# State attention with a gated projection: the scale of the scores moved into the exponentials, the order of all work remade

## Chip, cores, metric

One Trainium2 chip, one of its cores. The metric is device time of one execution in microseconds (us). The kernel before: 211.58 us, the median of 3 runs (211.08 to 211.69).

## What is computed

x is (8 batches, 8 heads, 512 tokens, 64), state is (8, 8, 32, 64), all in float32. Cut to what matters:

```python
scores  = (x @ state.T) / 8;  a  = softmax(scores);   xread = a  @ state     # per token, over 32 states
scores2 = (state @ x.T) / 8;  a2 = softmax(scores2);  sread = a2 @ x         # per state, over 512 tokens
x = concat([xread, sread], token axis)            # (8, 544, 512) after the heads are put side by side
gate = sigmoid(5-tap causal convolution of x over tokens, one weight per channel and tap)
out  = (gate * (x @ w_val)) @ w_out
```

(The reference's shapes give 512 + 32 tokens for each batch; `x` in the third line is reused for the concatenation.)

## The kernel before

Everything of one batch follows the same stages, and the stages of eight batches are interleaved. For batch b:

- `scores` (L347): PE multiplies the state, transposed (`sT`), with the tokens, transposed (`xT`), into two PSUM tiles `sc` (one for each half g of the heads). Each is 8 products on small parts of the array; a product in plain float32 leaves two records in the trace.
- The softmax over states: DVE transposes blocks of `sc` into `sl` (L400), takes the maximum `mx` (L410); POOL subtracts it (L221, `sl<-sl,mx`); ACT takes the exponential into `ex` (L417); DVE sums (`sm`) and inverts (`rc`); POOL multiplies (L221, `ex<-ex,rc`); DVE transposes back (L432) into `sl` (`a` for batch 0).
- The softmax over tokens: DVE takes the negated maximum `nb` straight from `sc` (`max_s`, L358); ACT takes `exp(sc + nb)` into `e2` (`exp_s`, L361). PE transposes `e2` (`exp_T`, tile `e2p`, L368), ACT or DVE copies it to `e2T`, PE multiplies with `x` (`state_read`, tile `srp`, L377), ACT divides (`sr`, L390), PE transposes (`srT`, L393) and ACT copies into `xt`, which the tail works on.
- `state_val` (tile `sgv`): state times `w_val` on PE, then `swh` and `swl`, a high and a low part that a fast matmul form can take. ACT makes the high part, DVE (`state_val_low`, L332) the low one.
- `read` (tiles `xr`, L439): PE makes the read of each of four channel groups; ACT, DVE and POOL make the five taps of the convolution (`acc`, `last`) and ACT the gate `sig`. For batch 0, PE does the taps (`read_conv`, L454, 80 records) from `z5`, which POOL makes from `z` and the taps.
- `values` (tiles `val`, L503): PE multiplies `ah`, `al` (high and low part of the softmax) with `swh`, `swl`. DVE makes `g = (sig + 1) * val` (L508), ACT or POOL its high part `gh` (L208, L212), POOL the low part `gl` (L221).
- `project` (tiles `op`, L512 to L514): three products of 512 columns for each of 4 x 4 pieces, with `woh` and `wol` (high and low part of `w_out`), copied to `o` and stored.

Weights arrive as float64 words; in the first 40 us ACT (`words_part` L279 `wt`, `words_side` L287 `ws`), POOL (`ws`, L289) and DVE (`words_sum`, L295 and L297; `words_join`, L304) turn them into float32, and ACT and POOL into `woh` and `wol`.

What the change is about: `sT`, the transposed state, is multiplied by 1/8 on ACT after it has landed (`state_T`, L316 to L318, three instructions), so that `sc` holds scaled scores, and the two places that use `sT` for `state_val` undo it with `HALF / SCALE` (L329, L333, L345).

```python
    def state_T(r, i0, i1):
        t = get("sT", r)[:, i0:i1]
        nc.scalar.mul(t, t, SCALE)
```

The order of the work is not left to a scheduler. The kernel lists its steps in `steps`; `ORDER` is a table of step numbers, in which a letter names the engine for steps that may run on ACT (a), DVE (v) or POOL (g). Each engine, and SP's DMA queue, runs its instructions in that order and waits in place. `SLOTS` names for each tile in turn the buffer that it takes; a buffer is written when its last reader is done, so a product on PE may wait for the engine that empties its PSUM tile (8 tiles, tag `ps`). `WARM` gives the numbers of filler products (`warm_up`, L314) at the start.

Of the kernel before, what the change touches and what calls it, by code (L numbers as in the profile page):

```python
# [8 lines left out]
F32 = mybir.dt.float32  # L9
F32R = mybir.dt.float32r  # L10
# [13 lines left out]
P = 128  # L24
# [5 lines left out]
PLAIN = (0,)  # L30
# [6 lines left out]
WARM = (9, 2, 14)  # L37
# [8 lines left out]
278 64a 146 168 288a 65g 147 279 187 135 274 129g 189 190 132a 275 133g 101 191 136 173a 148 193 276g 142 194 102a
199a 237 195 198 149 192a 200 137 196g 201 143 277 152 174g 197 153 284 205 202 154 144a 175 150a 155 207 138a 203g
219 208 156a 139 225 213a 209 151 226 282g 212 157 220 227 206a 214 238 204 221 215 285 228 294 210g 222 229a 216 378
223a 297a 217g 180 485 295a 380 181 145 286a 387 290 224g 182 389 289 388 298 183 239 184a 230g 218 379 231 291 232
240 390 299 283g 296 241a 381 211 292 233 293a 394 307 234 334 300 242g 309 328 395a 346 302 321 335 382g 310 329 301a  # L50
340 311 341 303 308a 347 336 323 383 312g 342 304 348 235a 324 243 305g 313 255 325 315a 384 330 236g 322a 256 314 244
326g 306 337 257 316 258 385g 331 245 393 332a 317 246 259a 318 333g 260 403 247a 386 377 338a 248 487 404a 339g 486
406a 396 703 489 327 249 319g 391a 498 250 405 499 251 392g 488 397a 252 349 320 407 261 253a 496 408 490 505 424a 343
262 506a 423 449 263 344a 425 264 345g 426 437 265a 427 438 409 352 428g 410a 439 416 411 450 491g 350a 353 412 497
354 418 429 364 419 351g 492 358 413 451 430 493 414g 365 417a 359 415 432 360 494g 433 366 420 361 431a 452 367 421g
362a 440 399 363 368a 434 398 495 112 435g 400 596 422 453a 512 812 605 441a 454g 369 597 401 515a 266 455 607 113a
456 500a 442g 355 516 436 598 443 606 501g 444 445 356a 457 402a 513a 446 357 503 608 458 517 447a 599 504a 614 448g
525 558 514 370 518 527 600g 532 461 615v 459a 371 528 533a 546 529 460g 372 534 526a 462 601 535 530g 547 536 373 520
467 537g 374a 502 564 521 375 559 538 560 539 468 561 519a 463 541 469 522 470 542 523g 464 540a 471a 507 543 465a 508
472 602 562a 544g 705 595 509 524 612 563g 706 929a 479 707 552 603g 714 548 510 553 549 554 716 550a 565 708 613a 566  # L60
551g 545 480 511a 611 715 473 604 531 481 567 474 609a 555 482 717 610g 475 927a 476 556a 483a 723 477a 621 484 557g
626 622a 709g 624a 623 617 634 625 616 724a 636 721 704 618 568g 655 478 627 637 667 466 641 629 656 569g 635a 588 630
710 668 631 589 722a 638 657 628a 643 619 669 933a 632g 661 644 931a 662 620a 711 663 639g 642a 590 633 591 720 648
712g 645 576 640 658 577 650 659a 726 646g 592a 651 725 664 814 727 813 660g 652 254 730 593 816 649a 815 728 731a 570
653g 823 729a 733a 571 825 824 572 817 826 573 647 713 578 665a 574a 579 666g 670 718a 735 734 580a 829 719g 732 830
736 581 832 671a 575 738 582 743 739 583 831a 818g 745 770 833a 771 654 740 673 757 746 584 737a 759 772 751a 741g 674
760 819 675 679 676 672g 742 764 744a 765 677a 691 747 750 761 766 748g 585 820 680 586a 678g 758a 692 752 749 681
762g 773 682 753 774a 685 821g 683a 767 693 754 684 768a 694 763 769g 822 839 695a 696 755g 835 827a 834 842a 844 775g
836 843 837 845 686 934g 852 687 847 840a 854 782 928g 756 783 848 838a 688 853a 841 828g 866 784 855 776 846a 785 777
689a 778 856 786a 690 697 937 779 587 857g 879 849 780a 891 938 868 892 932g 935a 885 869 880 860a 939 873 850g 858  # L70
886 881 787g 851 893 859 698 867a 936g 699 882 861 874 700 862 794 870 701a 781g 875 887 806 930g 876 807 863 877a
883a 788 940 878g 948 795 947 789 884g 950 942 941 871g 808 864g 949 943 952 944 951 872 953 945a 946g 800 954 801 894
955a 790 865 956g 796 921 895g 888 802 809 889a 896g 797 810a 922 890g 811 702 791 963 792a 957 909 803 958 804a 798a
964 799 965 793 923 805 966 959 967a 903 968 904 924 905 897 960 898 961a 910 925a 899 926 915 962 900 906 901a 911
902 907a 912 916 908 913a 917 918 914 919a 920
# [4 lines left out]
    "06126005634267501024315671027614305672465276124300127146753231763245041567746302041372520631672135460573642014"  # L80
    "375631520132715604234721237631500675123420124710253601714572056031437240534",
    x="0100101000",
    xT="01001001",
# [5 lines left out]
    ah="01001100101",
    al="0110011010",  # L90
    swh="0100110010",
    swl="011001101",
    acc="0120201221022011210102101202",
    last="0110100101011010011110110101",
    sig="00123323332233223333223332323322303",
    g="0101100110101001111010100101010101",
    gh="0011201100232231045210364126403514620153640",
    gl="01023121120345203164024361034261305241",
    o="0123030312111312320301003123020130",
    nb="00000000",  # L100
    r2="00100000",
    mx="00000000",
    sm="00000000",
    rc="00000000",
# [6 lines left out]
def state_attention_gated_kernel(  # L111
# [41 lines left out]
        sr=(1, [P, P], F32), sl=(2, [P, NG, S], F32),  # L153
# [3 lines left out]
        g=(2, [P, S], F32), gh=(7, [P, S], F32R), gl=(7, [P, S], F32R), o=(4, [P, C], F32),  # L157
        nb=(4, [P, NG], F32), r2=(2, [P, NG], F32),
# [33 lines left out]
    def op(fn, *args):  # L192
        steps.append((fn, args))
# [150 lines left out]
    def state_val_high_part(e, b, g, i):  # L344
        scale(e, get("sw0", b)[:, g, i * C // 2:(i + 1) * C // 2], get("sgv", b, g, i)[:, :C // 2], HALF / SCALE)  # L345
# [70 lines left out]
    def exp_n(b, i):  # L416
        nc.scalar.activation(part(ex, b, i)[..., :NS], blocks(get("sl", b), b, i), AF.Exp)  # L417
# [208 lines left out]
    def batch(b):  # L626
# [171 lines left out]
```

## Time and profile before

| what | value |
|---|---|
| median of 3 runs | 211.58 us |
| the profiled execution, its own time | 212.08 us |
| its span, first to last instruction | 209.9 us |
| PE busy | 203.2 us, 97% of the span, 1781 matmul records |
| DVE, ACT, POOL busy | 159.4, 155.2, 152.5 us (76%, 74%, 73%) |
| granted PE clock, mean | 0.997 of full speed |
| moved by DMA | 31.24 MB, 149 GB/s |

Matmul records overlap: the next one starts while the last one drains, and the ends are modelled. A product of 512 columns in the fast form has a duration of about 0.39 us, yet the next one starts some 0.23 us after it. So what PE can do is read from start to start, and a short wait shows as a longer step, not as idle time. ACT, DVE and POOL columns are plain busy time.

### The profile page before, as it was taken

To read this page: it belongs to the slowest core of one execution; us is meant where nothing else is said; L and a number is where in the kernel's file an instruction comes from. 1 tells how busy PE (TensorE), PEld (TensorE's weight loads), DVE (VectorE), ACT (ScalarE), POOL (GpSimd) and SP (SyncE) were. 2 spreads that over 40 slices of the span, in tenths; PEclk is the share of its full clock that TensorE was granted. 3 is DMA by queue.
4 is the path that set the end of the run, shared out by engine and by line. 5 is a ranking of instruction groups with operands and counts; after the bars stand their busy time and mean duration, and the time that the engine had idled before them with its cause. 6 is when DMAs were issued, how large, how long until landed. Compare 5 with 4: busy or idle time off the path is not lost.

```text
span 209.9 us, 4603 instructions
## 1 busy us (share of the span) xinstructions
PE 203.2 (97%) x1781; PEld 147.0 (70%) x1781; DVE 159.4 (76%) x255; ACT 155.2 (74%) x325; POOL 152.5 (73%) x118
## 2 busy tenths in 40 slices
PE   7799999999999999999999999999999999999994
PEld 6654457676688567766777857577866788988883
DVE  1799999998999988998969759998895988630000
ACT  3498999977987978789755989799879964333123
POOL 2286999999979938988938596948799999473000
PEclk9999999999999999999999999999999999999998
DMA  6999689604700692048016028182011200002525
GB/s 182 417 370 425 263 248 425 284 0 153 253 0 2 187 415 100 0 101 303 0 55 250 3 62 279 25 286 103 0 52 53 101 0 3 0 0 100 186 79 188
DMA packets 9507, 31.24 MB, mean 149 GB/s; under 512 B 1146, under 2 KB 1678, under 8 KB 7566
## 3 DMA queue, kind: packets, MB, share of 16 engines
q1 hardware_dynamic: 9342, 30.43, 39.9%
q10 hardware_dynamic: 144, 0.52, 1.0%
q8 instruction: 14, 0.23, 0.4%
q14 instruction: 7, 0.06, 0.1%
HBM read 22.04 MB, written 8.91 MB: 147 GB/s over the span
## 4 chain that ended last, share of the span: by engine, by line
PE 86%; DVE 4%; issue 1%; ACT 1%; ACTq 0%
PE val L503 21%; PE op L512 13%; PE op L514 13%; PE op L513 13%; PE srp L377 4%; PE e2p L368 4%; PE xr L439 3%; PE sgv L324 3%; PE tval L580 3%; PE sc L353 3%; DVE acc L483 2%; PE xr L454 2%; PE top L513 1%; PE top L514 1%; PE top L512 1%
## 5 line engine op out<-in xcount | busy, mean ns | idle before, releaser
L483 DVE SCALAR_TENSOR_TENSOR acc<-xr,cwt,acc 128x511 f32<-128x511 f32 (+2 forms) x84 | 60.3, 741 | 6.0 <-ACT last L216 2.4
L512 PE MATMUL op<-woh,gh 128*128 128x512 f32 x124 | 50.1, 404 | 0.2 <-DVE acc L483 0.2
L514 PE MATMUL op<-woh,gl 128*128 128x512 f32 x124 | 49.1, 396 | 0.0
L513 PE MATMUL op<-wol,gh 128*128 128x512 f32 x124 | 48.9, 394 | 0.0
L221 POOL TENSOR_TENSOR gl<-g,gh 128x512 fp32r<-128x512 f32 x32 | 41.2, 1295 | 7.7 <-ACT gh L208 7.5
L221 POOL TENSOR_TENSOR acc<-acc,last 128x508 f32<-128x508 f32 x28 | 35.9, 1286 | 12.8 <-DVE acc L483 7.0
L512 PEld LDWEIGHTS op<-woh,gh 128*128 128x128 f32 x124 | 23.4, 189 | 6.3 <-issue 0.6
L514 PEld LDWEIGHTS op<-woh,gl 128*128 128x128 f32 x124 | 23.3, 188 | 5.6 <-POOL gl L221 0.3
L513 PEld LDWEIGHTS op<-wol,gh 128*128 128x128 f32 x124 | 23.3, 188 | 5.0 <-issue 0.2
L208 ACT CAST gh<-g 128x512 fp32r<-128x512 f32 x30 | 18.7, 632 | 10.1 <-DVE g L508 8.0
L208 ACT COPY o<-op 128x512 f32<-128x512 f32 (+1 forms) x33 | 18.4, 579 | 10.1 <-PE op L514 8.3
L508 DVE SCALAR_TENSOR_TENSOR g<-sig,val 128x512 f32<-128x512 f32 x32 | 21.3, 675 | 5.7 <-POOL tgl L221 1.5
L216 ACT ACTIVATE last<-xr,cwt 128x508 f32<-128x508 f32 x28 | 19.7, 708 | 6.5 <-DVE acc L483 5.0
L221 POOL TENSOR_TENSOR sl<-sl,mx 128x1024 f32<-128x1024 f32 (+1 forms) x9 | 15.6, 1729 | 7.3 <-DVE mx L410 7.2
L495 ACT ACTIVATE sig<-acc 128x512 f32<-128x512 f32 x28 | 17.9, 641 | 2.6 <-POOL acc L221 2.6
L478 ACT ACTIVATE acc<-xr,cwt 128x512 f32<-128x512 f32 x28 | 19.3, 708 | 0.7 <-PE xr L439 0.5
L221 POOL TENSOR_TENSOR al<-sl,ah 128x1024 fp32r<-128x1024 f32 x7 | 16.9, 2413 | 2.5 <-ACT ah L208 2.3
L503 PE MATMUL val<-ah,swh 128*128 128x512 f32 x56 | 17.2, 403 | 0.0
L503 PE MATMUL val<-al,swh 128*128 128x512 f32 x56 | 17.1, 395 | 0.0
L503 PE MATMUL val<-ah,swl 128*128 128x512 f32 x56 | 16.7, 397 | 0.4 <-issue 0.4
L221 POOL TENSOR_TENSOR ex<-ex,rc 128x1024 f32<-128x1024 f32 (+1 forms) x9 | 15.6, 1729 | 1.6 <-DMA z<-z_in 0.9
L332 DVE SCALAR_TENSOR_TENSOR swl<-sgv,swh 128x512 fp32r<-128x512 f32 x14 | 9.3, 676 | 5.5 <-ACT swh L216 5.5
(120 smaller groups left out, 378.3 us busy)
## 6 DMA issues: line engine op xcount, KB each, us to landing
x<-x_in SPq DMA_DIRECT2D x8, 1024.0 KB, 7.2
out<-o SPq DMA_DIRECT2D x31, 256.0 KB, 2.3
xT<-xT_in SPq DMA_DIRECT2D x7, 1024.0 KB, 10.9
vw<-w_val SPq DMA_DIRECT2D x4, 511.8 KB, 9.4
ow<-w_out SPq DMA_DIRECT2D x4, 511.8 KB, 5.2
xT<-xT_in ACTq DMA_DIRECT2D x1, 512.0 KB, 4.8
xT<-xT_in SPq DMA_DIRECT2D x1, 512.0 KB, 5.3
z<-z_in SPq DMA_DIRECT2D x2, 256.0 KB, 7.9
```

The source lines that it names most:

```text
L208: nc.scalar.copy(out, in_)
L216: nc.scalar.mul(out, in_, factor)
L221: (nc.vector if e == "DVE" else nc.gpsimd).tensor_tensor(out, a, b, op=how)
L332: nc.vector.scalar_tensor_tensor(get("swl", b)[:, g], get("sgv", b, g), HALF / SCALE, get("swh", b)[:, g].bitcast(F32), op0=ALU.mult, op1= ...
L478: nc.scalar.mul(get("acc", b, pr), pt, cw[:, HALO, pr:pr + 1])
L483: nc.vector.scalar_tensor_tensor(acc[:, d:], get("xr", b, pr)[:, :S - d], cw[:, HALO - d, pr:pr + 1], acc[:, d:], op0=ALU.mult, op1=ALU.add)
L495: nc.scalar.activation(get("sig", b, pr), get("acc", b, pr), AF.Tanh, scale=0.5)
L503: nc.tensor.matmul(get("val", b, k), w[:, g, c], a[:, g], start=(term == 0 and g == 0), stop=(term == terms - 1 and g == NG - 1))
L508: nc.vector.scalar_tensor_tensor(get("g", b, k), get("sig", b, k), 1.0, get("val", b, k), op0=ALU.add, op1=ALU.mult)
L512: nc.tensor.matmul(pt, gh, woh[:, k], start=(k == 0), stop=False)
L513: nc.tensor.matmul(pt, gh, wol[:, k], start=False, stop=False)
L514: nc.tensor.matmul(pt, gl, woh[:, k], start=False, stop=(k == NPR - 1))
```

## The change

- The three multiplications of `sT` go. `sc` now holds unscaled scores; both exponentials on ACT take `scale=SCALE` (1/8) with their input, and the three uses of `HALF / SCALE` become `HALF`.
- The exponential over tokens needs its bias scaled as well: a new step `bias_s` makes `ns = nb / 8`, one value for each partition, two for each batch. The table puts 13 of these 16 steps on POOL and 3 on DVE.
- `SLOTS` gives the buffers nearly always in turn; `sr` has 2 buffers instead of 1, `g` 3 instead of 2, `o` 8 instead of 4, and `ns` 4.
- On SP's queue the weight loads ahead of `x` of batch 0 come in the order `vw` 3, `ow` 3, `vw` 2, `ow` 0; before it was `ow` 3, `ow` 0, `vw` 3, `vw` 2.
- `ORDER` is remade throughout. The 25 filler products, before in groups of 9, 2 and 14, stand in groups of 9, 2, 5, 6, 1 and 2.

```diff
-WARM = (9, 2, 14)
+WARM = (9, 2, 5, 6, 1, 2)
...
-68 15 0 8 69 20 25 158 2 6 1 55 40 9 969 71 10a 35 11 74 73 12 75 970 72 30 81 13 76g 14a 82 22a 91 70 77 83 21 78 84g
...
+65 12 0 5 66 17 22 157 1 3 32 52 982 68 6 7a 27 71 70 8 72 983 69 37 9 79 73g 78 18 89 67 74 80 984 10 15 90g 11a 16a
...
-    sr="00000000",
-    sl="00101010",
+    sr="01010101",
+    sl="01010101",
...
-        sr=(1, [P, P], F32), sl=(2, [P, NG, S], F32),
+        sr=(2, [P, P], F32), sl=(2, [P, NG, S], F32),
...
-        g=(2, [P, S], F32), gh=(7, [P, S], F32R), gl=(7, [P, S], F32R), o=(4, [P, C], F32),
-        nb=(4, [P, NG], F32), r2=(2, [P, NG], F32),
+        g=(3, [P, S], F32), gh=(7, [P, S], F32R), gl=(7, [P, S], F32R), o=(8, [P, C], F32),
+        nb=(4, [P, NG], F32), ns=(4, [P, NG], F32), r2=(2, [P, NG], F32),
...
-    def state_T(r, i0, i1):
-        t = get("sT", r)[:, i0:i1]
-        nc.scalar.mul(t, t, SCALE)
-
...
-        scale(e, get("sw0" if b in PLAIN else "swh", b)[:, g], get("sgv", b, g), HALF / SCALE)
+        scale(e, get("sw0" if b in PLAIN else "swh", b)[:, g], get("sgv", b, g), HALF)
...
+    def bias_s(e, b, g):
+        c = slice(g, g + 1)
+        (nc.vector if e == "DVE" else nc.gpsimd).tensor_scalar_mul(get("ns", b)[:, c], get("nb", b)[:, c], SCALE)
+
     def exp_s(b, g):
         nc.scalar.activation(
-            get("e2", b, g), get("sc", b, g), AF.Exp, bias=get("nb", b)[:, g:g + 1],
+            get("e2", b, g), get("sc", b, g), AF.Exp, bias=get("ns", b)[:, g:g + 1], scale=SCALE,
             accum_out=sum2[:, b, g, 0:1])
...
-        nc.scalar.activation(part(ex, b, i)[..., :NS], blocks(get("sl", b), b, i), AF.Exp)
+        nc.scalar.activation(part(ex, b, i)[..., :NS], blocks(get("sl", b), b, i), AF.Exp, scale=SCALE)
...
             op(max_s, b, g)
+            op(bias_s, b, g)
             op(exp_s, b, g)
...
         op(load_state_T, r, i0, i1)
-        op(state_T, r, i0, i1)
```

Three places show how the instructions moved. The first is DVE at the start of the program (`sl`, `mx`, `nb`: batch 0's scores transposed, their maxima; `wt_conv`, `cv`: the convolution weights). Before:

```order
L295 TENSOR_TENSOR wt_conv<-wt_conv,ws_conv 20x128
L400 STREAM_TRANSPOSE sl_142<-sc_1_129 128x256
L400 STREAM_TRANSPOSE sl_142<-sc_0_127 128x256
L304 SCALAR_TENSOR_TENSOR cv<-cww,wt_conv 20x128
L410 TENSOR_REDUCE mx_146<-sl_142 128x2x8
L400 STREAM_TRANSPOSE sl_142<-sc_0_127 128x256
```

The same place on DVE after the change:

```order
L402 STREAM_TRANSPOSE sl_140<-sc_1_126 128x256
L402 STREAM_TRANSPOSE sl_140<-sc_0_124 128x256
L297 TENSOR_TENSOR wt_conv<-wt_conv,ws_conv 20x128
L412 TENSOR_REDUCE mx_144<-sl_140 128x2x8
L306 SCALAR_TENSOR_TENSOR cv<-cww,wt_conv 20x128
L402 STREAM_TRANSPOSE sl_140<-sc_1_126 128x256
```

The join of the convolution weights stood ahead of the first two transposes and now stands behind them.

The second is POOL from the step that makes `gl` for batch 0 on (`ns`: the new small step; `wol`: the low part of `w_out`; `sl<-sl,mx`: the subtraction for batch 2). Before:

```order
L221 TENSOR_TENSOR gl_1_427<-g_1_378,gh_1_409 128x512
L221 TENSOR_TENSOR ex<-ex,rc_407 128x32x32
L221 TENSOR_TENSOR wol<-wc_o_391,woh 128x512
L221 TENSOR_TENSOR gl_0_508<-g_0_471,gh_0_499 128x512
L221 TENSOR_TENSOR wol<-wc_o_501,woh 128x512
L221 TENSOR_TENSOR sl_434<-sl_434,mx_510 128x1024
L221 TENSOR_TENSOR wol<-wc_o_542,woh 128x512
L221 TENSOR_TENSOR gl_2_569<-g_2_515,gh_2_532 128x512
```

The same stretch of POOL after the change:

```order
L223 TENSOR_TENSOR gl_0_465<-g_0_381,gh_0_445 128x512
L360 TENSOR_SCALAR ns_492<-nb_481 128x1
L223 TENSOR_TENSOR gl_1_500<-g_1_409,gh_1_484 128x512
L360 TENSOR_SCALAR ns_492<-nb_481 128x1
L223 TENSOR_TENSOR ex<-ex,rc_449 128x32x32
L223 TENSOR_TENSOR wol<-wc_o_515,woh 128x512
L223 TENSOR_TENSOR sl_502<-sl_502,mx_530 128x1024
L223 TENSOR_TENSOR gl_2_564<-g_2_524,gh_2_547 128x512
L223 TENSOR_TENSOR wol<-wc_o_553,woh 128x512
L223 TENSOR_TENSOR gl_3_596<-g_3_545,gh_3_562 128x512
```

The two small steps of batch 2 stand between the `gl` steps, each behind a maximum that DVE takes; the pieces of `gl` come in the order of their channel groups.

The third is PE at the state reads of batches 1 and 2 (`srp`, `srT`: read and its transpose; `sr`: what ACT makes between them; `e2p`: the transposes of batch 2's exponentials; `val`: a large product of batch 1). Before:

```order
L377 MATMUL srp_745<-x_430,e2T_0_374 32x64 x16
L377 MATMUL srp_745<-x_430,e2T_1_525 32x64 x16
L377 MATMUL srp_788<-x_480,e2T_1_555 32x64 x16
L377 MATMUL srp_788<-x_480,e2T_0_784 32x64 x16
L393 MATMUL srT_831<-ident,sr_807 128x128
L503 MATMUL val_3_614<-ah_600,swl_563 128x512 x2
L503 MATMUL val_2_841<-ah_600,swh_518 128x512 x2
L503 MATMUL val_2_841<-al_640,swh_518 128x512 x2
```

The same place on PE after the change:

```order
L379 MATMUL srp_746<-x_385,e2T_1_513 32x64 x16
L379 MATMUL srp_746<-x_385,e2T_0_427 32x64 x16
L370 MATMUL e2p_0_790<-ident,e_2_0_538 128x128 x4
L505 MATMUL val_3_802<-ah_590,swh_535 128x512 x2
L395 MATMUL srT_811<-ident,sr_797 128x128
L505 MATMUL val_3_802<-al_612,swh_535 128x512 x2
L505 MATMUL val_3_802<-ah_590,swl_570 128x512 x2
L379 MATMUL srp_828<-x_443,e2T_1_555 32x64 x16
L379 MATMUL srp_828<-x_443,e2T_0_821 32x64 x16
```

The read of batch 2 no longer follows that of batch 1 at once; its transposes and large products stand between a read and the transpose `srT`.

## Rows read from the trace of the kernel before

**Rows 1.** Table by stretch: busy us of each engine, granted clock, DMA share, GB/s

```profile
core 0: us, PE busy (x) PEld busy (x) DVE busy (x) ACT busy (x) POOL busy (x), PEclk, DMA share, GB/s
0.00:16.40 16.40, 13.32 (x134) 10.19 (x134) 10.33 (x23) 9.74 (x21) 7.36 (x20) 1.00 0.88 326
16.40:37.30 20.90, 20.89 (x241) 10.98 (x241) 20.56 (x33) 20.40 (x42) 18.76 (x14) 1.00 0.89 340
...
57.90:207.00 149.10, 148.76 (x1155) 111.90 (x1153) 109.75 (x171) 107.12 (x224) 106.96 (x74) 1.00 0.29 100
```

**Rows 2.** PE in order of time: large products around a group of small ones

```profile
36.73 0.40 PE L513 MATMUL op<-wol,gh 128*128 128x512 f32 x1
36.96 0.39 PE L514 MATMUL op<-woh,gl 128*128 128x512 f32 x1
37.28 1.11 PE L439 MATMUL xr<-sl,z 32*64 32x512 f32 x16
38.33 0.33 PE L393 MATMUL srT<-ident,sr 128*128 128x128 f32 x1
38.41 0.48 PE L512 MATMUL op<-woh,gh 128*128 128x512 f32 x1
38.73 0.40 PE L513 MATMUL op<-wol,gh 128*128 128x512 f32 x1
```

**Rows 3.** Source line L318 and ACT in order of time: start us, us, what

```profile
L318 ACT ACTIVATE sT<-sT x3: 309/511/662, 4.7 to 34.4; 128x128 f32<-128x128 f32 x1, 128x384 f32<-128x384 f32 x1, 128x512 f32<-128x512 f32 x1
...
10.11 1.36 ACT L279 ACTIVATE wt_v<-vw,edge 128x512 f32<-128x512 int16 x2
```

**Rows 4.** PE in order of time: the first scores

```profile
5.61 0.67 PE L353 MATMUL sc<-xT,sT 64*32 64x256 f32 x16 [0.88 <-DMA xT<-xT_in]
```

**Rows 5.** Groups by line and shape: the smallest steps on POOL and DVE

```profile
L787 POOL MEMSET const-float32-1.0<- 128x1 f32 x1 | 0.1, 107 | 0.0
...
L385 DVE RECIPROCAL r<-r 128x2 f32<-128x2 f32 x8 | 1.3, 166 | 0.3
```

**Rows 6.** DVE in order of time, start and batch 1's softmax

```profile
6.60 0.29 DVE L295 TENSOR_TENSOR wt_conv<-wt_conv,ws_conv 20x128 int32<-20x128 f32 x1 [4.65 <-ACT ws_conv L287]
...
14.95 1.30 DVE L432 STREAM_TRANSPOSE a<-ex 128x512 f32<-128x512 f32 x2
...
35.09 1.22 DVE L432 STREAM_TRANSPOSE sl<-ex 128x1024 f32<-128x1024 f32 x1
```

**Rows 7.** PE in order of time: batch 0's read with its taps

```profile
16.40 4.54 PE L454 MATMUL xr<-a,z 32*64 32x512 f32 x80
```

**Rows 8.** POOL in order of time: batch 0's taps, a weight word

```profile
14.55 1.60 POOL L221 TENSOR_TENSOR z<-z,cwb 128x640 f32<-128x640 f32 x1
...
20.13 1.98 POOL L289 TENSOR_SCALAR ws_v<-vw 128x512 f32<-128x512 int16 x1 [1.89 <-DMA vw<-w_val]
```

**Rows 9.** PE's weight loads during batch 0's first value products

```profile
22.22 0.19 PEld L503 LDWEIGHTS val<-a,sw 128*128 128x128 f32 x1 [0.24 <-issue]
23.25 0.30 PEld L503 LDWEIGHTS val<-a,sw 128*128 128x128 f32 x2 [0.84 <-ACT sig L474]
23.78 0.19 PEld L503 LDWEIGHTS val<-a,sw 128*128 128x128 f32 x1 [0.24 <-issue]
```

**Rows 10.** PE in order of time: state read of batches 1 and 2, srT

```profile
53.66 0.33 PE L393 MATMUL srT<-ident,sr 128*128 128x128 f32 x1
54.35 0.62 PE L503 MATMUL val<-ah,swl 128*128 128x512 f32 x2 [0.36 <-issue]
```

**Rows 11.** PE in order of time: a wait among the projections

```profile
103.57 0.40 PE L514 MATMUL op<-woh,gl 128*128 128x512 f32 x1
104.14 0.47 PE L512 MATMUL op<-woh,gh 128*128 128x512 f32 x1 [0.17 <-DVE acc L483]
```

**Rows 12.** PE in order of time: srT of batch 6

```profile
136.50 0.33 PE L393 MATMUL srT<-ident,sr 128*128 128x128 f32 x1
136.90 0.50 PE L512 MATMUL op<-woh,gh 128*128 128x512 f32 x1
```

More of the change, by code (lines that the diff above doesn't have):

```diff
@@ L46 @@
[L46 to L75, printed above, removed]
+65 12 0 5 66 17 22 157 1 3 32 52 982 68 6 7a 27 71 70 8 72 983 69 37 9 79 73g 78 18 89 67 74 80 984 10 15 90g 11a 16a
@@ new lines @@
+75 19a 81g 268 24a 86 76g 82 20 985 13 23 83 87g 14a 986 159 25 88 84g 21 91 93 108g 26 95 94a 77 102 96a 85 34g 104a
+103a 168 987 109 33 171 53 161 54a 172g 169g 160 29g 173 35 170 162 39a 36 38 163g 177 55 113 117 115 40 114 56 28 41
+121 42 63g 30 57a 47 118 116 158 58g 379 164 31 98 122 97 178a 64g 92 105 269 119a 165 270 99 106a 120g 44a 186 490
+282 107a 123a 179 279 283g 43 133 124g 272 125 45 284 280g 271 166g 180a 46 49a 290 126 59a 129 273 48 60g 187a 50 281
+139 274g 130 127a 145 51 291a 146 189a 167 131a 128g 134 61a 188 140 275 62g 190 191 174a 276 132g 100 141 192 147
@@ new lines @@
+200a 194 175g 101a 142 287 195 220 143a 148 196 206 144 226 199 277g 208 135 149a 201 227 193a 150 209 221 197g 232
+202 222 176 233 203 198 228 278 214a 151 204g 213 234 223 152 110g 205 215 153 207a 216 285a 136 210 154 229 211g 297
+155a 217 137a 381 230a 218g 138 212 182 601 393 300a 181 286g 156 298a 390 288 491 183 301 238 2 219 383 184 4 239
+224a 240 382 289a 391g 394g 225g 293 185a 235 392 292 299 395 302 380 231g 384 294 295 310 399 241 385g 337 296a 312
+304a 331 303 349 313 350 242a 305 332 311a 243g 338 400a 314 339 324 343 306 315g 236a 351 307 344 333 326 316 308g
@@ new lines @@
+345 386 327 244 340 237g 245 309 387 318a 256 325a 250 317 328 257 388g 319 258 320 259 334 329g 246 260a 321 341a 247
+389 335a 322g 492 330 248a 408 712 504 336g 323 249 494 401 409a 251 493 505g 411a 402a 346 252 506 410 253 396a 412
+413 352 347a 397g 501 254a 512 428 262 414 263 430 421 264 431 348g 415a 265 502v 495 429a 342g 454 266a 455 423 503
+456 432 367 424 433g 442 361 425 416 443 496g 422a 444 398 434 362 435 457 368 417 353a 355 458a 354g 418 497 363 509
+437 369 419g 513a 438 370 498 364 371a 436a 448 356 420 439 499g 404 445 403 111 405 519 112v 365a 426g 500 603 366
@@ new lines @@
+520a 267 440g 427 372 406 604 357 522a 261 521 407a 460 823 446a 449 615 602 507a 450 605 358 616v 508g 612 461 359a
+451 510 617 606 373 511a 462 452a 523 447g 524 441 623 539 459g 463 374 525 541 375 533a 613g 453g 542 472 532 543
+624a 376 607g 527 614 473 534 540a 553 464a 535 565 544g 377a 566 536 466 378 465g 545 360 554 567 546 474 537g 608
+548 467 526a 468 528 555 549 484 529 469 550 514 530g 470a 568 515 471 714 609 516 547a 517 538 559 551g 726 485 531
+942a 716 571 727g 610g 569a 572 556 518a 475 946a 715 560 476a 621 611 557a 573 552 561 558g 486 562 487 570g 723 478
@@ new lines @@
+574 488a 717 724g 563a 479 489 618a 564g 480 481 622a 725 619g 630 482v 728 635 633a 631a 634 626 636 575g 632 625 643
+638 734 713 940a 732 645 477 576g 735a 676 483 620 733a 677 646 255 650 718g 664 639 595 644a 640 627 665 666 647 637a
+596 652 719 641g 628 670 653 597 731 648g 642 720 671 651a 672 657 678 598 654 649 721g 659 736 599a 737 629a 660 825
+738 824 673 655g 600 667 741 661 656 739 583 834 740a 658a 722 584 668a 662g 577 744a 679 742a 578 835g 826 674a 579
+729a 827 585 745 663 730g 586 837 836 743 580 587a 828 746 588 581a 680a 582 838v 843 747 681g 682 844a 749 683 755a
@@ new lines @@
+781 829g 750 768 684 775 751 839 776 770 754 845 669g 748a 782 771 783 756 752g 589 685 777 757 700 675g 753 758 846a
+590 830 842 591 759g 772 688 686a 778 769a 831 592 687g 761 694 760 773g 689 593a 784 762a 701 594 832g 779a 763 702
+785a 690 764 774 703 944a 780g 833 691 765 786g 847 692a 848 704a 693 852 849 943g 705 840a 857 855a 766g 850 856 865
+695 841g 859a 793 867 851a 794 767 868 795 858 787 869 853a 788 796 866a 789 854 696 879 870g 790 904 860 892 941g 871
+893 881 791a 886 861 905 951 947g 697 862 887 953 698a 863g 894 872 699 706 948a 792g 707 874 898 882 708 949g 873a
@@ L76 @@
+895 797a 888 906 883 896a 709 875 880a 899 945g 710a 876 900 950 817 711 864 952 798g 818 961 960 955 897g 889 954 956
+963 884g 877g 811 885 890a 799 907 891g 962 966 908a 878 909g 965 957 964 901 805 967 800 958a 819 959g 812 806 813
+902a 801 903g 807 922 968a 916 969g 923 814 970 815a 802 820 808 971 809a 803a 972 821a 804 934 816 935 822 976 977
+936 937 978 973 979 974a 928 980a 910 938a 981 917 911 912 939 918 810 975 913 919 914a 924 920a 915 925 929 921 926a
+930 927 931 932a 933
 """.split()
@@ L79 @@
     ps=
[L80 to L83, printed above, removed]
+    "71207073475473612407215704630547503461507240523540611253012467361567214013450601725714523634062714571034641205"
+    "375216246507510273640150174271230407356404217036453407213150136467231070421672",
+    x="0101001000",
+    xT="01010101",
     sT="01",
-    e2="0001000111020202",
-    e2T="0120122102101001",
-    sr="00000000",
-    sl="00101010",
[L89 to L104, printed above, removed]
+    e2="0120102102102101",
+    e2T="0121012010201202",
+    sr="01010101",
+    sl="01010101",
+    ah="01001010101",
+    al="0101010101",
+    swh="0100101010",
+    swl="010101010",
+    acc="0120210210210210120120121021",
+    last="0110011001101001011010010110",
+    sig="01230132013201302130210320132013201",
+    g="0120120121010212012102112012021021",
+    gh="0123456012346513024615034261035461203546120",
+    gl="01234561045236104253160452310642351064",
+    o="0123456701325170423571064235710634",
+    nb="01230123",
+    ns="01230123",
+    r2="01001010",
+    mx="01010101",
+    sm="01010101",
+    rc="01010101",
     z5="0",
@@ L328, in state_val_high @@
     def state_val_high(e, b, g):
-        scale(e, get("sw0" if b in PLAIN else "swh", b)[:, g], get("sgv", b, g), HALF / SCALE)
+        scale(e, get("sw0" if b in PLAIN else "swh", b)[:, g], get("sgv", b, g), HALF)
     def state_val_low(b, g):
         nc.vector.scalar_tensor_tensor(
-            get("swl", b)[:, g], get("sgv", b, g), HALF / SCALE, get("swh", b)[:, g].bitcast(F32),
+            get("swl", b)[:, g], get("sgv", b, g), HALF, get("swh", b)[:, g].bitcast(F32),
             op0=ALU.mult, op1=ALU.subtract)
@@ L344, in state_val_high_part @@
     def state_val_high_part(e, b, g, i):
-        scale(e, get("sw0", b)[:, g, i * C // 2:(i + 1) * C // 2], get("sgv", b, g, i)[:, :C // 2], HALF / SCALE)
+        scale(e, get("sw0", b)[:, g, i * C // 2:(i + 1) * C // 2], get("sgv", b, g, i)[:, :C // 2], HALF)
     def scores(b, i):
```

4 lines of the change are left out of this document (removed).

## The prediction

> **What bounds the kernel now.** I read the table by stretch first. PE is busy for 20.89 of 20.90 us from 16.40 on, and for 148.76 of 149.10 from 57.90 to 207 [rows 1]. So PE's own stream sets the end. DVE and ACT matter only where they make PE wait. They are nearly full from 16.40 to 37.30, 20.56 and 20.40 of 20.90, while in the long stretch behind they have over a quarter free [rows 1].
>
> Both kernels issue the same products; what differs is where they stand and which waits lie between them. A busy PE hides short waits, since records overlap; so I read PE's rows from start to start and compare with a row of the same kind that waits for nothing. A large product is 0.23 us behind the one before it (36.73 to 36.96), and `srT` takes 0.08 before the next starts (38.33 to 38.41) [rows 2]. What is over these is a wait or the edge of a group. The four largest waits from 16.4 us on are shown below and come to 0.27 + 0.61 + 0.34 + 0.32 = 1.54 us. They are nearly all that another order of the same work can win there.
>
> **The change part by part.**
>
> *The scaling of `sT`.* Three instructions on ACT of 309, 511 and 662 ns go, 1.48 us [rows 3]. I book nothing. ACT has 149.10 − 107.12 = 42 us free in the long stretch. The first of the three starts at 4.7 and takes 0.31 us [rows 3], yet the scores it feeds start only at 5.61, when the tokens land [rows 4]; the cover is that load. If the cover were gone, the gain would be the first instruction's 0.31.
>
> *`ns`.* Sixteen steps of 128x1, 13 on POOL, 3 on DVE. Nothing in the trace has just this form. From below, a fill of the same shape on POOL takes 0.107 us, and a reciprocal of two columns on DVE 0.166 [rows 5]. From above, the smallest join on DVE (20x128) takes 0.29 [rows 6]. I take 0.17: 2.7 us in all, against POOL's 149.10 − 106.96 = 42 us free. Nothing on PE's path, between 0 and 0.3. What it does add is a new link, from the maximum on DVE over POOL to the exponential on ACT, with the exponential queued behind POOL's other work; that belongs to a rival below. Exponentials with a scale are the same instruction with another constant: 0.
>
> *The start.* Before, DVE waits 4.65 us for ACT's `ws_conv` and starts the join at 6.60, with the first transposes of scores behind it [rows 6]. In the new order these come first and can start when the scores are there, at 5.61 + 0.67, about 6.3 [rows 4]. But batch 0's read with taps, at 16.40 [rows 7], also needs `z`, which POOL makes from 14.55 to 16.15 [rows 8]. So of the earlier start only some 0.2 can arrive. The upper bound is −0.4. From the other side, ACT has more small work ahead of the second `ex` and no pair of `wt_v` of 1.36 us [rows 3]; that leaves +0.3 possible. I take **−0.2**.
>
> Here the filler products stand in smaller groups. The granted clock in the first stretch is 1.00, the upper level of 2.4 GHz, with PE busy for 13.32 of 16.40 us [rows 1], filler included; the number of filler products stays 25, so I book 0. The Trainium skill ("TensorE: Matmul & The Clock Gate", "What's actually happening") says that the default state is throttled and that activity releases it. By that rule thinner filler could bring the clock down, and the sum would end 4.5 higher (the clock rival); no row here shows a fall.
>
> *Batch 0's first value products.* A weight load follows the one before it by 0.19 + 0.24 = 0.43 us. From 22.22 to 23.78 there are three such steps, 1.29, but 1.56 pass: 0.27 of waiting for ACT's `sig` [rows 9], which frees the PSUM tile. The new order gives each `val` a tile that is free sooner: **−0.27**. If instead a `sig` is late, the same wait could grow to +0.6 (one ACT instruction of 0.63 to 0.68 is the nearest size).
>
> *The state read of batch 1.* `srT` takes 0.69 to the next start (53.66 to 54.35) [rows 10] against 0.08 [rows 2]: 0.61 goes, since two `sr` buffers and a large product stand between `srp` and `srT`: **−0.61**. In return the next state read stands right behind `e2T`, whose copy ACT makes: between 0 and 0.6 (the wait it replaces). I take **+0.25**, a little under half, because large products of 0.23 each stand ahead of it.
>
> *From 57.9 us on.* Two waits go: 103.57 to 104.14, a step of 0.57 against 0.23, so 0.34, for DVE's `acc` [rows 11]; and 0.40 against 0.08, so 0.32, at `srT` of batch 6 [rows 12]. Together **−0.66**. A new order of eight batches through eight PSUM tiles makes new ones; in three places a product now reuses a tile only two or three large products (0.23 each) behind its last reader's input, where ACT or POOL must have copied it out. Bounds: 0, and 1.5 (two waits as large as the one at `srT` of batch 1, one like that of `acc`). I take **+0.4**, a single one of the size of that for `acc`, nearest since it is of this stretch and kind.
>
> *Groups of small products.* The edges of a group cost: the last large product before takes 0.32 (36.96 to 37.28) and the first behind 0.32 (38.41 to 38.73) where 0.23 is normal, so 0.18 a group [rows 2]. The listed order has 19 such groups against 17, as the state reads of two batches are torn apart: **+0.36**, between 0.15 and 0.6.
>
> *Sum:* −0.2 − 0.27 − 0.61 + 0.25 − 0.66 + 0.4 + 0.36 = −0.73. The profiled execution took 212.08 us (span 209.9 and 2.2 around it, which stays), so 211.35; it stands 0.5 over the median of 211.58. On the median: **210.85**.
>
> **The rivals.**
>
> *Waits only move (no change).* Everything PE waited for was less than 1% of the time, and the new order can make as many waits as it takes. With +1.15 for new ones in place of +0.65 and the start at 0: 211.58 − 0.73 + 0.5 + 0.2 = 211.55. For it: the 1.48 us taken off ACT were never on PE's path. Against it: the waits that go are named, the new ones are not. This is also the case that the change doesn't do what it says.
>
> *No new waits.* Without the +0.25 and +0.4: 210.2. Against it: tiles are reused sooner in places.
>
> *Slower: DVE held up at batch 1's softmax.* DVE runs 32 instructions between the transposes of `a` at 14.95 and the end of `sl` at 35.09 + 1.22 = 36.31 [rows 6], all but full; the read of batch 1 on PE starts at 37.28 [rows 2], about 0.97 later, some 0.5 if PE itself comes 0.47 earlier (the start and the first value products). POOL waited 1.89 us for a weight in this stretch [rows 8]. If a weight comes as late in the new load order, POOL's `ws_v`, the `ns` behind it and DVE's join all wait in place, and DVE has no free time to regain it. PE then waits 1.89 − 0.5 = 1.4: 210.85 + 1.4 = 212.25. It decides from DVE being late by 0.5 + 0.73, about 1.2 us. Against it: `vw` 3, which POOL wants first, is now loaded two places sooner.
>
> *Slower: the clock.* If the thinner filler let the clock fall to 1.2 GHz while the taps run, the 4.54 us of [rows 7] would take twice that: about 215.3. The granted clock is 1.00 in all three stretches shown [rows 1], so it is unlikely.
>
> **How the numbers follow.** Anything under 0.3%, 0.63 us, can't be told from no change, so faster means below 210.95 and slower above 212.2. The forecast's case (210.3 to 211.2) has 0.44; its centre lies just under the bound, so 0.31 of that is faster and 0.13 same. No new waits: 0.14, faster. Waits only move: 0.24, of which 0.04 end above 212.2. DVE held up: 0.15, of which 0.11 over the bound, since a shorter delay stays under it. Clock: 0.03. Together faster 0.45, same 0.37, slower 0.18. The range begins at the best bounds (start −0.4, no new waits, groups +0.15): −0.4 − 0.27 − 0.61 − 0.66 + 0.15 = −1.8, so 209.8. It ends at 212.5, just over the DVE rival, and leaves out the clock and the worst of the held-up cases.
>
> **What would show it.** Right: `srT` of batch 1 followed within 0.1 to 0.3 us; no step over 0.5 at the `op` products; the read with taps of batch 0 at 16.0 to 16.4; PE busy all but 1 us from there on; the last product some 0.7 us earlier. Wrong: PE standing before the read of batch 1 with DVE as releaser; a step over 1 us at a `srp`; a granted clock under 0.9 anywhere before 207; POOL's `ns` just ahead of a late exponential with `e2p` behind it.

## The result and the profile after

| | changed | before | ratio |
|---|---|---|---|
| median, in us | 212.81 (7 runs, 212.34 to 214.18) | 211.55 (7 runs, 211.08 to 211.81) | 1.0085 (95%: 1.0062 to 1.0107) |
| the same pair again, on another occasion | 213.08 (6 runs, 212.31 to 214.30) | 211.38 (12 runs) | 1.0087 (1.0061 to 1.0112) |
| profiled execution | 212.81, span 210.8 | 212.08, span 209.9 | |

The change makes the kernel slower by 0.85%, about 1.3 to 1.7 us between the medians. The forecast was 0.73 faster. The changed kernel also spreads more: its runs lie from 212.3 to 212.8 and near 214, those of before within 0.7 us (of 91 later runs of before, two lie above 213 all the same, at 213.52 and 214.16). The two profiled executions are only 0.7 us apart, because that of before stands 0.5 above its median.

The table by stretch of the changed kernel, with the columns of [rows 1]:

```profile
core 0: us, PE busy (x) PEld busy (x) DVE busy (x) ACT busy (x) POOL busy (x), PEclk, DMA share, GB/s
0.00:16.40 16.40, 14.04 (x130) 10.42 (x131) 10.09 (x22) 9.10 (x19) 7.59 (x22) 1.00 0.88 330
16.40:37.30 20.90, 20.90 (x242) 12.08 (x241) 20.44 (x34) 20.48 (x42) 19.69 (x17) 1.00 0.92 367
57.90:207.00 149.10, 148.62 (x1148) 110.34 (x1148) 109.93 (x175) 107.42 (x225) 106.22 (x78) 1.00 0.29 101
```

PE is as busy as before, so this table does not tell where the time went. The chain of waits does. Of the changed kernel, the chain of the first 17 us in order of time (start, us, what):

```profile
1.16 4.41 DMA cww<-conv_w
...
5.64 1.28 ACT L281
...
6.93 0.37 ACT wt_conv L281
7.30 0.35 ACT ws_conv L289
...
7.67 0.04 DVE wt_conv L297
...
7.88 0.68 DVE mx L412
...
8.70 1.06 POOL sl L223
```

The second piece has no tile name. ACT in order of time shows what it is, of before and then of the changed kernel:

```profile
1.17 1.28 ACT L318 ACT_TABLE_LOAD   x1 [1.17 <-PEq L787]
4.73 0.31 ACT L318 ACTIVATE sT<-sT 128x128 f32<-128x128 f32 x1 [2.28 <-DMA sT<-sT_in]
5.86 0.40 ACT L279 ACTIVATE wt_conv<-cww,edge 20x128 f32<-20x128 int16 x1 [0.82 <-DMA cww<-conv_w]
```

```profile
5.64 1.28 ACT L281 ACT_TABLE_LOAD   x1 [5.64 <-DMA cww<-conv_w]
6.93 0.37 ACT L281 ACTIVATE wt_conv<-cww,edge 20x128 f32<-20x128 int16 x1
```

In each of these traces ACT loads its function table once, ahead of its first activation. Before, that was the first multiplication of `sT`; the load ran at 1.17 us, while the data were on their way. With that multiplication gone, the first activation is `wt_conv`, and the load stands **behind** the wait for the convolution weights (5.64). Its 1.28 us now follow the arrival of the data. The list of instructions with their waits (a semaphore's name says which engine or DMA queue it belongs to) says so for both kernels, before and changed:

```
2 L318 ACT_TABLE_LOAD
3 L318 ACTIVATE sT_97<-sT_97 128x128 [waits DMAHW1_49]
4 L279 ACTIVATE wt_conv<-cww,edge 20x128 [waits DMAHW2_49,Pool_49]

2 L281 ACT_TABLE_LOAD [waits DMAHW2_49]
3 L281 ACTIVATE wt_conv<-cww,edge 20x128 [waits Pool_49]
```

`wt_conv` waits for two things, its data and POOL's fill of `edge`. The changed list has the first of the two on the table load; in the trace too the load is released by the arrival of `cww`, and `wt_conv` follows it without a wait. The Trainium skill ("ScalarE: Activation LUTs", "What ACT_TABLE_LOAD costs") gives about 1283 ns for one load; the trace agrees with 1.28 us.

PE in order of time at the places of the prediction, changed kernel:

```profile
16.85 4.64 PE L456 MATMUL xr<-a,z 32*64 32x512 f32 x80
...
21.92 3.60 PE L505 MATMUL val<-a,sw 128*128 128x512 f32 x8
...
37.43 1.11 PE L441 MATMUL xr<-sl,z 32*64 32x512 f32 x16
...
53.81 0.27 PE L395 MATMUL srT<-ident,sr 128*128 128x128 f32 x1
53.84 0.70 PE L505 MATMUL val<-al,swh 128*128 128x512 f32 x2
...
102.29 0.40 PE L516 MATMUL op<-woh,gl 128*128 128x512 f32 x1
102.87 0.50 PE L505 MATMUL val<-ah,swh 128*128 128x512 f32 x1 [0.18 <-ACT e L363]
...
163.99 0.40 PE L516 MATMUL op<-woh,gl 128*128 128x512 f32 x1
164.69 0.50 PE L505 MATMUL val<-ah,swh 128*128 128x512 f32 x1 [0.30 <-DVE swl L330]
```

The read with taps starts 0.45 later than in [rows 7]. By the read of batch 1 PE is only 0.15 behind [rows 2]. `srT` of batch 1 is followed after 0.03 [rows 10]. Two new waits stand at 102.29 (step 0.58 for 0.23) and 163.99 (0.70 for 0.23).

The same kernel profiled on the other occasion (212.31 us) has the late load and the same two waits, steps of 0.57 and 0.67, but its read with taps starts at 16.48, only 0.08 later than in [rows 7]. So the waits go with the kernel, and the 0.45 at the start varies from run to run.

### The profile page after: what moved, and what is told of

It reads as the page before. It is cut to its first block, busy times and chain, and to the rows that moved or that the text cites. A ratio compares the mean times of both kernels' runs of the same rounds, so it can differ in the third digit from the quotient of the medians.

```text
span 210.8 us, 4611 instructions
## 1 busy us (share of the span) xinstructions
PE 204.9 (97%) x1781; PEld 147.5 (70%) x1781; DVE 159.4 (76%) x259; ACT 155.0 (74%) x323; POOL 150.9 (72%) x129
## 4 chain that ended last, share of the span: by engine, by line
PE 88%; ACT 5%; DMA 2%; DVE 2%; issue 1%; POOL 1%; SPq 0%; POOLq 0%; ACTq 0%
PE val L505 21%; PE op L514 13%; PE op L516 13%; PE op L515 13%; PE srp L379 4%; PE e2p L370 4%; PE xr L441 4%; PE sgv L322 3%; PE tval L582 3%; PE sc L351 3%; PE xr L456 2%; DMA cww<-conv_w 2%; ACT acc L480 1%; DVE acc L485 1%; PE top L515 1%; PE top L514 1%
## 5 line engine op out<-in xcount | busy, mean ns | idle before, releaser
L210 ACT CAST gh<-g 128x512 fp32r<-128x512 f32 x31 | 19.4, 636 | 2.5 <-PE op L515 2.2
L505 PE MATMUL val<-ah,swh 128*128 128x512 f32 x56 | 18.0, 414 | 0.5 <-DVE swl L330 0.3
L402 DVE STREAM_TRANSPOSE sl<-sc 128x512 f32<-128x512 f32 (+1 forms) x18 | 10.9, 632 | 4.3 <-PE sc L351 4.3
```

The lines of the kernel that those rows point to most:

```text
L210: nc.scalar.copy(out, in_)
L402: nc.vector.transpose(get("sl", b)[:, g, tokens(b, i)], get("sc", b, g)[:, tokens(b, i)])
L505: nc.tensor.matmul(get("val", b, k), w[:, g, c], a[:, g], start=(term == 0 and g == 0), stop=(term == terms - 1 and g == NG - 1))
```

## The experiments

Theory A: the late table load is the loss. Theory B: the waits of the new order are.

**1. The table load first.** One 128x1 multiplication is put first on ACT; nothing else changes. The same edit is in every later run "with the table load first".

```diff
+    tick = const.tile([P, 1], F32, name="tick")
+    def first_table():
+        nc.scalar.mul(tick, blank[:, :1], SCALE)
```

> The changed kernel with one 128x1 multiplication put first on ACT, so that the table load (1.28 us) no longer stands behind the arrival of the convolution weights. Theory A (the lost table load opens the chain at the start): the table load starts near 1.2 instead of 5.64 us, wt_conv starts when its data lands near 5.6 to 5.9, batch 0's read with taps starts at 16.2 to 16.4 instead of 16.85, and the kernel is 0.4 to 1.2 us faster than the changed kernel: 211.6 to 212.4, ratio to before 1.000 to 1.004. Theory B (the waits of the new order alone): the start moves but PE loses it again before 37 us; ratio stays 1.006 to 1.011.

Measured: 211.46 us (12 runs, 211.30 to 213.53), ratio 1.0019 (0.9987 to 1.0050). Eight of the runs lie at 211.30 to 211.62, four at 212.8 to 213.5. So a 128x1 multiplication takes back nearly all of the loss, 1.35 us between the medians, and the intervals of the two ratios do not overlap; theory B falls. The load is back at its place (ACT in order of time):

```profile
1.16 1.28 ACT L347 ACT_TABLE_LOAD   x1 [1.16 <-PEq L794]
2.45 0.20 ACT L347 ACTIVATE tick<-blank 128x1 f32<-128x1 f32 x1
5.88 0.37 ACT L282 ACTIVATE wt_conv<-cww,edge 20x128 f32<-20x128 int16 x1 [3.23 <-DMA cww<-conv_w]
```

The profiled run was one of the upper four (213.53 us). PE in order of time there, and the same instructions of the changed kernel:

```profile
5.78 1.11 PE L355 MATMUL sc<-xT,sT 64*32 64x256 f32 x16 [0.53 <-DMA xT<-xT_in]
6.82 1.22 PE L317 MATMUL warm<-blank 128*128 128x128 f32 x4
7.97 1.11 PE L355 MATMUL sc<-xT,sT 64*32 64x256 f32 x16
9.01 2.02 PE L317 MATMUL warm<-blank 128*128 128x128 f32 x10
10.96 0.23 PE L274 MATMUL cwtp<-ident,cv 20*128 20x20 f32 x1
...
17.98 4.64 PE L460 MATMUL xr<-a,z 32*64 32x512 f32 x80
```

```profile
5.31 0.67 PE L351 MATMUL sc<-xT,sT 64*32 64x256 f32 x16
5.91 0.71 PE L316 MATMUL warm<-blank 128*128 128x128 f32 x4
6.91 0.67 PE L351 MATMUL sc<-xT,sT 64*32 64x256 f32 x16 [0.30 <-DVE sl L402]
7.51 1.38 PE L316 MATMUL warm<-blank 128*128 128x128 f32 x10
8.89 0.20 PE L273 MATMUL cwtp<-ident,cv 20*128 20x20 f32 x1
```

The same products take 1.11 for 0.67 us, and the fillers hold `cwtp` back to 10.96. The read with taps starts at 17.98, not at the 16.2 to 16.4 expected, and that is most of the 2.1 us by which this run lies over the lower eight. The granted clock reads 1.00 there all the same, because the clock's record in this trace begins only at 10.38 us (at 4.04 in that of before) and the column shows 1.00 where there is none; only the durations tell the lower pace.

**2. The order alone.** `sT` is scaled on ACT as before, no `ns`; order, buffers and filler are the new ones.

> The new order, buffers and filler, but the scaling of sT kept on ACT and no ns steps. Theory A: the first sT multiplication again takes the table load to the front, so it is like the run with the table load first, ratio 1.000 to 1.004. Theory B: like the changed kernel, 1.006 to 1.011.

Measured: 213.15 us (12 runs), ratio 1.0075 (1.0043 to 1.0107). The number is theory B's, the trace is neither's: the table load is early (1.17 us), but the three `sT` steps stand where I put them, and one holds PE (PE in order of time):

```profile
13.64 0.66 PE L353 MATMUL sc<-xT,sT 64*32 64x512 f32 x8 [0.74 <-ACT sT L236]
```

The read with taps then starts at 16.92. That wait is not all of the time lost, so this run does not separate the order from the edit.

**3 and 4. The scale alone, in the order of before.** `ns` on POOL just ahead of each exponential; the second run adds the 128x1 multiplication.

```diff
-        op(state_T, r, i0, i1)
...
-    bias=get("nb", b)[:, g:g + 1],
+    bias=get("ns", b)[:, g:g + 1], scale=SCALE,
```

> The order and buffers of before, but the scale moved into the exponentials, sT not multiplied, ns on POOL right ahead of each exponential. Theory A: the table load waits for the convolution weights here too (start near 5.6 us), batch 0's read with taps starts 0.5 to 1 us later than 16.40, ratio 1.002 to 1.006. Theory B: ratio 0.998 to 1.001, since ACT only loses work.

> The run with the scale alone moved, plus the 128x1 multiplication first on ACT. Theory A: the loss of the run without it goes, ratio 0.997 to 1.001. Theory B: the same as the run without it within 0.1%.

Measured: 219.97 us, 1.0384 (1.0338 to 1.0429), and 218.24 us, 1.0308 (1.0266 to 1.0350). The early load gives 1.7 us here too, but both theories had forecast about the time of before with it, and both missed: the other 6.7 us neither had. The view of the tile `ns` in the second run names them:

```profile
L450 POOL TENSOR_SCALAR ns<-nb x16: 198/216/228, 11.9 to 144.3; 128x1 f32<-128x1 f32 x16
...
  ACT e L453: 8.5, 10
```

A step of 0.216 us, for which ACT's exponential waited 8.5 us in ten waits, since it stands in POOL's queue behind steps of 1.3 to 1.9 us.

**5 and 6. `ns` on DVE right behind each maximum, in the order of before,** with the table load first and then without.

> The order of before with the scale moved, the table load first, and ns on DVE right behind each maximum instead of on POOL. Theory E (the loss of the run with the scale alone, 6.7 us, is ACT's exponentials waiting 8.5 us for ns in POOL's queue): most of it goes, 211.5 to 213.5. Rival (the loss is ACT's own order without the sT steps, or the exponential): stays above 216.

> The run with ns on DVE in the order of before, without the 128x1 multiplication first on ACT: the table load waits for the convolution weights again. Theory A (the late table load costs 0.8 to 1.4 us in any order): 213.0 to 213.6 against 212.15 with it early. Theory B (it costs only what the new order makes of it): 212.0 to 212.5.

Measured: 212.15 us, 1.0037 (1.0018 to 1.0056), and 213.59 us, 1.0120 (1.0092 to 1.0148). Theory E holds: 6 of the 6.7 us go. The engine and the place in the queue changed together, so which of the two did it is not shown. And the late load costs 1.44 us between the medians in the old order as well (these two ran on different occasions; their ratios to before differ by 0.83%). In the profile of the second one, at 215.07 us the slowest of its six runs, PE waits 1.96 us for DVE ahead of the second scores, and the granted clock then falls to its lower level of 1.2 GHz (table by stretch: PE busy, granted clock, DMA share, GB/s; then PE in order of time):

```profile
7.00:8.00 1.00, 0.00 (x0) 1.00 1.03 422
8.00:9.00 1.00, 0.08 (x8) 0.61 1.09 455
9.00:10.00 1.00, 1.00 (x17) 0.50 0.97 410
...
14.00:15.00 1.00, 1.00 (x6) 0.50 1.04 426
15.00:16.00 1.00, 1.00 (x9) 0.97 1.03 422
```

```profile
8.92 1.11 PE L436 MATMUL sc<-xT,sT 64*32 64x256 f32 x16 [1.96 <-DVE sl L487]
```

So the clock rival of the prediction exists, though the fall came after an idle PE, not with thinner filler. The rule of the Trainium skill cited there ("TensorE: Matmul & The Clock Gate", "What's actually happening") agrees with this row: 0.50 after a stretch with no product.

**7 and 8. What makes the upper runs: PE's pace?** The table load first, and either the group of five fillers moved behind `cwtp` and the first `cwbp`, or 12 fillers instead of 9 at the start.

> The kernel with the table load first, and the group of five filler products moved behind the transpose of the convolution weights (cwtp) and the first cwbp product. Theory C (the upper cluster of the times, 212.8 to 213.5 us, comes from starts in which PE stays at its lower pace, a filler step of 0.213 instead of 0.112 us, past the first scores; the five fillers then hold cwtp back by about 1 us): the runs near 211.4 stay, the upper cluster moves down by 0.7 to 1.1 us, to 211.9 to 212.6. Rival D (the upper cluster comes from the arrival of data or from elsewhere): both clusters stay where they are.

> The kernel with the table load first, and 12 filler products instead of 9 ahead of the first scores. Theory C: PE reaches its faster pace before the first scores in more of the starts, so fewer runs lie above 212.5 us (before 4 of 12), the others at 211.4 to 211.7 as the first scores may start up to 0.3 us later. Rival D: 4 of 12 above 212.5 as before, and all the others 0 to 0.3 later.

Measured: 211.71 us (12 runs, 211.41 to 213.30), 1.0015 (0.9993 to 1.0038); and 211.60 (211.40 to 212.53), 1.0014 (0.9993 to 1.0035). In the first, one run lies over 212.5; in the second, four at 212.31 to 212.53 stand apart from eight at 211.40 to 211.87. So the upper runs come lower, as theory C forecasts. Yet the first one's highest, 213.30, is the profiled one, and PE was at its faster pace there from 5.57 us on. ACT in order of time shows another cause:

```profile
26.61 0.39 ACT L219 ACTIVATE sw<-sgv 128x256 f32<-128x256 f32 x1
29.06 0.76 ACT L290 ACTIVATE ws_o<-ow,edge 128x512 f32<-128x512 int16 x1 [2.06 <-DMA ow<-w_out]
```

ACT stands in place for the weight block `w_out` 1, and PE waits behind it, 0.70 us at `e2p` and 0.57 at `val`. The load of that block needs the buffer of `w_out` 3, which DVE frees; in the new order DVE does so later. SP's queue of before, then of the changed kernel, where the load of `w_out` 1 is issued:

```profile
21.08 0.33 SPq L248 DMA_DIRECT2D ow<-w_out  x1
```

```profile
23.07 0.93 SPq L250 DMA_DIRECT2D ow<-w_out  x2
```

In the profiles of runs 7 to 9 the issue comes at 22.4 to 22.5, still 1.3 to 1.4 us later than before, while ACT comes to the block sooner, here at 27.0 for 27.5. How long the transfer then takes differs: issued at 22.49 it was there by 26.90 in run 8, issued at 22.44 it let ACT start only at 29.06 here.

**9. The two late products.** The table load first; ACT's exponential of batch 5 ahead of a copy, batch 7's `swh` and `swl` ahead of an `acc` and a `g`.

> The kernel with the table load first, and two moves in the order: ACT's exponential of batch 5 ahead of the copy of e2T (the product at 102.87 us waited for it), and batch 7's swh and swl ahead of an acc and a g (the product at 164.69 waited for swl). If the two late products are the rest of the loss: 0.34 + 0.10 and 0.47 + 0.10, about 0.9 us faster at best, 210.5 to 210.9 for the lower cluster. If PE meets the next wait instead: 211.1 to 211.5.

Measured: 211.25 us (12 runs, 210.97 to 211.89), 0.9994 (0.9976 to 1.0013). Inconclusive alone; run 13 repeats the moves with run 12 beside it. Its profile (211.89) starts the read with taps at 15.74, the soonest of all, and loses that again: ACT waits 1.01 us for `w_out` 1 and starts `ws_o` at 27.84, and PE comes to the read of batch 1 only at 37.45, for 36.89 in run 12.

**10 and 11. `w_out` 1 sooner, and all together.** In the first, DVE finishes `w_out` 3 ahead of `w_val` 3 and `w_out` 0; the second adds 12 fillers and the two moves.

> The kernel with the table load first, and on DVE the two steps that finish w_out 3 (wt_o, wc_o) ahead of the steps that finish w_val 3 and w_out 0, so that its buffer is free and w_out 1 is loaded about 1.6 us sooner (issue near 20.8 instead of 22.4 us). Theory F (the runs above 212 come from ACT waiting 1 to 2 us for w_out 1 near 27 us, as two profiles show): at most 2 of 12 runs above 212.2, median 211.2 to 211.5. Theory C (they come from PE's pace at the start): 3 or 4 of 12 above 212.5 as in the first run with the table load first.

> The table load first, 12 filler products ahead of the first scores, w_out 3 finished sooner, and the two moves of the exponential of batch 5 and of batch 7's swh and swl. If each removes what it was seen to remove: 210.4 to 210.9 median, all under 211.6, faster than before by 0.2 to 0.4%. If the next wait takes their place: 211.0 to 211.5.

Measured: 211.99 us (6 runs, 211.85 to 212.20), 1.0029 (1.0018 to 1.0040); and 212.42 (211.95 to 213.41), 1.0055 (1.0035 to 1.0076). Both medians lie above what was expected. No run of the first lies over 212.20, but all its runs are some 0.5 us slower: `w_val` 3, now later, holds a PSUM tile that `val` needs. PE's waits in the first name it (us in total, times, longest), and the second has the same row (its further 0.4 us is not explained):

```profile
PE val L509 <- DVE wv L307: 0.5, 1, 0.5
```

**12 and 13. Room for `w_out` 1 without that price.** The table load first; `w_out` 3 ahead of `w_out` 0 only, and ACT's `ws_o` of block 1 two steps later in its queue. The second run adds the two moves.

```diff
-... 55 113 117 115 40 114 56 28 41 ... 120g 44a 186 490 282 107a 123a 179 279 283g 43
+... 55 113 117 115 56 40 114 28 41 ... 120g 186 490 282 107a 123a 179 279 283g 44a 43
```

> The kernel with the table load first; w_out 3 finished one step sooner on DVE (ahead of w_out 0 only, so w_val 3 is not delayed), and ACT's ws_o of w_out 1 two steps later in its queue. Theory F (the runs above 212 come from ACT standing in place for w_out 1 near 27 us): one PE-slow start aside, all runs 211.2 to 211.7, none of the 1 to 2 us between 28 and 33 us. Theory C (they come from PE's pace at the start): 3 to 4 of 12 above 212.5.

> The same, with the two moves of the exponential of batch 5 and of batch 7's swh and swl. If both hold: median 210.7 to 211.1, ratio 0.996 to 0.999, the first version under both kernels. If the next waits take their place: 211.1 to 211.5, ratio 0.999 to 1.001.

Measured: 211.40 us (11 runs, 211.26 to 211.83), 1.0007 (0.9998 to 1.0015); and 211.37 (211.12 to 211.58), 1.0001 (0.9992 to 1.0010). No run of the 22 lies over 211.83, as theory F forecasts. That alone does not show it: run 9 without the room has none over 211.89, though ACT waited 1.01 us there. What the profiles show is one upper run of each kind, PE's pace in run 1 and `w_out` 1 in run 7. With the room ACT no longer waits in place (ACT in order of time, the first of the two):

```profile
27.25 0.65 ACT L211 CAST gh<-g 128x512 fp32r<-128x512 f32 x1
27.76 0.82 ACT L290 ACTIVATE ws_o<-ow,edge 128x512 f32<-128x512 int16 x1
```

The two late products also shrink by themselves once the table load is early (PE in order of time, same run):

```profile
101.76 0.40 PE L520 MATMUL op<-woh,gl 128*128 128x512 f32 x1
102.03 0.73 PE L509 MATMUL val<-ah,swh 128*128 128x512 f32 x2
...
163.12 0.39 PE L520 MATMUL op<-woh,gl 128*128 128x512 f32 x1
163.53 0.50 PE L509 MATMUL val<-ah,swh 128*128 128x512 f32 x1
```

Steps of 0.27 and 0.41 in place of 0.58 and 0.70. It is the early load and not the room that does it: in the profiles of runs 1, 2, 7 and 8, without the room, the second step is 0.37 to 0.39 and the first under 0.31 as well, even where the read with taps starts later (17.98 and 16.92 in runs 1 and 2) than in the changed kernel. The moves bring nothing beyond that which can be measured. No version beats the kernel before by more than its interval.

## Why the prediction was wrong

- *The scaling of `sT`*: this step failed. "I book nothing", with a gain of 0.31 if the cover were gone. That ACT's 1.48 us lie off PE's path was right. But the edit took away ACT's first activation, to which the table load was tied, and the load moved to 5.64 us, behind data. Putting an activation back first gives 1.35 us (new order), 1.44 (old order, `ns` on DVE) and 1.73 (`ns` on POOL), all between medians. That is about the whole measured loss, 1.26 and 1.70 us. The load stood in the trace of before as a row of ACT, at 1.17 us, and I costed instructions removed without asking what else hung on the first of them.
- *`ns`*: my 0.17 us was near (0.213 on POOL in the changed kernel, 0.154 on DVE in run 5). "Nothing on PE's path" holds only in the remade order: in the order of before the kernel was 6.7 us over before with it on POOL and 0.8 with it on DVE. So the scale could not be moved without moving the steps around it.
- *The start*: −0.2 forecast, with +0.3 as the worst; +0.45 came in one profile of the changed kernel and +0.08 in the other, both with the late load. With the load first it starts at 16.31 in run 12 (−0.1) and at 15.74 in run 9 (−0.7), so "only some 0.2 can arrive" was too low a bound; the 0.7 was lost again at `w_out` 1.
- *First value products*: −0.27 forecast; 3.60 for 3.88 us, −0.28.
- *State read of batch 1*: −0.61 forecast; −0.66 came (0.03 for 0.69). The new wait for `e2T`, +0.25, did not: no step of that kind in the trace.
- *From 57.9 us on*: the two old waits went as forecast. The new ones were mis-sized: 0.35 and 0.47, with some 0.1 behind each, about 1.0 where I took 0.4. Some 0.6 of this goes with the late table load, since it is gone in every profile with the early one (runs 1, 2, 7, 8, 12). PE itself had nearly caught up by 37 us; that ACT and DVE had not is likely, but the way from 5.64 us to these two waits was not followed.
- *Groups*: mis-sized. The edges are there, at 0.09 each, but there are more of them than two groups make. From 34 us on, steps of 0.30 to 0.36 from one large product to the next number 16 before and 22 in the changed kernel (23 in run 12), without those behind the two late waits, and steps of 0.32 or 0.33 into a small group number 9 and 12. That is some 0.8 to 0.9 us for +0.36.
- *The rivals*: DVE held up at batch 1's softmax did not happen (`sl` ends at 36.66, the read starts at 37.43). Its mechanism, a weight that comes late in the new order and an engine that stands in place for it, did appear, on ACT at `w_out` 1, through a buffer freed 1.3 to 2 us later. The clock rival did not decide the changed kernel's profiles, but run 6 shows it at work. And "the granted clock in the first stretch is 1.00" was a misreading: the record of that trace begins at 4.04 us, and the first fillers before it step by 0.213 us, those behind it by 0.112.

With both faults mended the new order is at 1.0007, some 0.15 us over before, where the sum of the other terms said about −0.7. Between the two profiles it is −0.39 (211.69 for 212.08), and the edges above, less the `e2T` wait that did not come, are about what is missing there. The rest, some 0.5 us, lies between profiles and medians: that of before stands 0.5 to 0.8 above its medians, that of run 12 only 0.3. The waits that I took away were read from that one profile, and I took it that every run of before has them. Which of them a run near the median lacks no trace shows, so this part stays open.

## What to carry to other kernels

When an instruction goes, look at what was tied to its place: the first activation on ACT brought the table load, and a 128x1 activation at the very start kept that load under the first transfers. Read the list of instructions with their waits for the first few rows of each engine, since a wait may sit on another instruction than the one that needs it. A new small step between two engines can cost far more than its length: sixteen steps of 0.2 us made the kernel 6.7 us longer from POOL's queue, and 0.8 on DVE right behind their inputs. And read a gain from a profile that lies near the median: this one lay 0.5 us above it.

## What the runs showed that I had not expected

- Kernels with the same products take 0.5 to 2 us more or less by what happens in the first 12 us, though PE is 97% busy and seems to set the end by itself.
- PE's first products ran at a lower pace while the granted clock read 1.00 (`sc` 1.11 for 0.67 us), as the clock's record had not begun; after PE was idle for 1.96 us, the column showed 0.50 for some seven us.
- The arrival of one weight block near 27 us differs by over 2 us between profiles of nearly the same kernel (26.90 or sooner, 27.84, 29.06 in runs 8, 9, 7), though it was issued within 0.1 us. ACT waited in place for it; two steps of room took that wait away.
